# Values, bits and logits in four 32-column tiles of the matrix engine, sums turned by block transposes, 12 code rows a head, and a new order

## The chip, the cores and the metric

The kernel runs on one core of a Trainium2 chip. The metric is the device time of one execution in microseconds (us); the median of three runs before the change is 448.5 us (448.18 to 450.23). One further execution was profiled, and all rows below are from it. The engines are PE (the matrix engine; PEld is its weight load), DVE (vector), ACT (scalar), POOL (GpSimd) and SP, whose queue issues all DMAs.

## The reference

The program is three stages on 2 x 8 heads of 768 tokens with 64 columns each.

```
# attention with hashed buckets, per head
q_bits, k_bits = (q @ proj > 0), (k @ proj > 0)        # 6 bits a token
mask   = bucket(q_bits) == bucket(k_bits)
scores = where(mask, q @ k.T / 8, -1e9)
attn   = softmax(scores);  out = attn @ v
# soft mixture of experts, x is 1536 x 512, 32 slots of 8 experts
logits = x @ phi                                       # softmax over tokens, and over slots
slots  = softmax(logits, axis 0).T @ x
slots  = relu(slots @ w1[e]) @ w2[e]
x      = softmax(logits, axis 1) @ slots
# feed-forward, 512 -> 2048 -> 512
h = x @ w_in;  out = (h * sigmoid(1.702 h)) @ w_out
```

## The kernel before

Attention is written as one long list of steps, the string `ATTENTION`. Each word names a function, a head, a block of 128 keys (or queries) and a half of 384 queries, and is issued in that order. Every engine takes its own instructions in the order in which they stand, so the list sets the order on all engines and on SP's queue. A second string, `MISC`, gives each small PSUM tile one of two banks. SP's queue holds the loads of raw (q and k of a head, transposed), v, the expert weights (w), pieces of w_in, and the small moves inside SBUF.

The steps of one head n are these.

- `bits` (L390) projects q and k on the six directions, fp32, into PSUM `bp`: two column tiles of 64, one a half of 384 tokens. For head 0 (L396) q and k are projected on their own. `bits2` (L379) makes code rows of it on DVE: a threshold, then a factor. `bits3` (L372) moves these rows by four DMAs of 32 x 384 from `Bt` into rows 64 to 95 of `QK2`. The codes are such that the product of the code rows of q and k adds a large negative number for every bit that differs. They take 24 rows, so that the product that uses them has 88 rows.
- `a` (L448) multiplies queries by keys with the code rows, and DVE takes the maximum of each query (L455). `mrow` and `mstore` (L488) bring these maxima into one more row of `QK2`.
- `c` (L496) and `s` (L504) add up the scores in PSUM from split high and low parts; `e` (L509) takes the exponential on ACT into P; `p` (L517) adds the P of the key blocks on POOL into `Ps`.
- `av` (L523) multiplies v by P, fp32: two column tiles of 64, one a half of queries. Six key blocks add up in PSUM.
- `sum` (L554) multiplies `Ps` by ones, four column tiles of 32 with 384 queries each for a pair of heads; ACT copies it (L558), `rec` (L563) turns it with three PE transposes, and DVE takes the reciprocals.
- `xtok`, `xp`, `xn` turn and scale the output into rows of x. `xT` turns x again, and `lg` (L655) multiplies it by phi: two column tiles of 32 with 384 tokens each for a pair, and DVE adds it into `LT` (L657, L659), where 64 partitions hold one batch's 768 tokens in two halves.

A product in fp32 shows as two records a tile; the record counts below are such. `spin` steps are products without use at the start. After the attention list the buffers of attention are given to further expert weights (L223), and the expert stage, at whose head the logits are put together (L773), and the feed-forward stage follow.

Of the kernel before, what the change touches and what calls it, by code (L numbers as in the profile page):

```python
# [47 lines left out]
a.1.0 p.0.2.0 hi2.2.0 av.0.0 e.0.2.1 e.0.1.1 c.0.5.0 c.0.4.1 a.1.1 s.0.4.1 win.1 w4.0 we.1.1 p.0.1.1 we.1.2 w1.1 raw.3
bits3.2 hi2.2.1 av.0.1 s.0.5.0 we.1.3 e.0.5.0 w2.1 a.1.2 w3.1 av.0.2 c.0.5.1 p.0.3.0 e.0.3.1 c.0.4.0 mr.1 hq.1 e.0.4.1
a.2.1 ms.1 s.0.4.0 bits.3 p.0.2.1 bits2.3 s.0.5.1 lo1.2.1 e.0.4.0 a.2.0 av.0.3 av.0.4 vs.1 hi2.3.1 mp.1 p.0.3.1  # L50
bits3.3 a.2.2 c.1.0.1 lo2.2.1 e.0.5.1 s.1.0.1 av.0.5 a.2.4 hi2.3.0 c.1.3.0 s.1.3.0 win.2 p.0.4.1 lo1.2.0 c.1.0.0
e.1.0.1 v.2 s.1.0.0 c.1.1.0 w4.1 s.1.1.0 e.1.3.0 avo.0 c.1.2.0 e.1.1.0 p.0.4.0 a.2.3 e.1.0.0 s.1.2.0 c.1.1.1 lo2.2.0
s.1.1.1 e.1.2.0 c.1.2.1 we.2.0 we.2.1 s.1.2.1 c.1.4.1 s.1.4.1 hi1.2.1 a.2.5 p.0.5.1 av.1.0 e.1.2.1 e.1.1.1 c.1.3.1
c.1.4.0 raw.4 p.1.1.0 mr.2 p.1.1.1 s.1.3.1 p.1.2.1 w1.2 s.1.4.0 w2.2 p.1.2.0 e.1.3.1 e.1.4.0 e.1.4.1 w3.2 a.3.4
lo1.3.0 av.1.1 p.1.3.0 av.1.2 av.1.3 lo1.3.1 a.3.5 c.1.5.0 s.1.5.0 c.1.5.1 p.0.5.0 hq.2 ms.2 s.1.5.1 e.1.5.0 c.2.0.0
s.2.0.0 hi2.4.1 e.1.5.1 lo2.3.0 we.2.2 c.2.1.1 hi1.3.1 a.3.1 av.1.4 lo2.3.1 w4.2 hq.3 p.1.3.1 bits.4 bits2.4 p.1.4.1
e.2.0.0 mp.2 a.3.2 c.2.1.0 p.1.4.0 s.2.1.0 s.2.1.1 e.2.1.0 phi c.2.5.0 av.1.5 e.2.1.1 avo.1 s.2.5.0 a.3.0 e.2.5.0
c.2.0.1 s.2.0.1 win.3 we.2.3 e.2.0.1 c.2.5.1 c.2.3.0 s.2.5.1 w1.3 e.2.5.1 raw.5 p.1.5.0 vs2.0 bits3.4 p.2.1.0 s.2.3.0
e.2.3.0 p.1.5.1 hi2.4.0 c.2.2.0 a.3.3 s.2.2.0 av.2.0 w2.3 av.2.1 bits.5 v.3 w3.3 nom.0 c.2.3.1 e.2.2.0 a.4.2 s.2.3.1
c.2.4.0 c.2.2.1 s.2.2.1 mr.3 e.2.3.1 s.2.4.0 c.2.4.1 p.2.1.1 s.2.4.1 e.2.2.1 p.2.2.1 a.4.3 av.2.2 p.2.2.0 vs.2 ms.3  # L60
lo1.4.0 av.2.3 e.2.4.0 e.2.4.1 av.2.4 hi2.5.0 bits2.5 av.2.5 c.3.1.0 a.4.0 we.3.0 hi1.4.1 s.3.1.0 lo2.4.0 e.3.1.0
c.3.0.0 sum.0 s.3.0.0 p.2.3.0 p.2.4.0 a.4.4 c.3.3.1 p.2.3.1 nom.1 w4.3 c.3.3.0 e.3.0.0 p.2.4.1 xtok.0 bits3.5 s.3.3.0
# [1213 lines left out]
```

## Time and profile before

| | |
|---|---|
| median of three runs | 448.5 us (448.18 to 450.23) |
| the profiled execution | 447.2 us, its span 445.4 us |
| PE busy | 433.7 us, 97% of the span |
| DVE busy | 306.0 us, 69% |
| ACT busy | 284.9 us, 64% |
| POOL busy | 218.9 us, 49% |
| DMA | 75.09 MB, mean 169 GB/s |

The span runs from the first to the last instruction; the rest of the execution's time lies around it. Attention ends near 241 us, the expert stage near 285, and the feed-forward stage takes the remainder. A busy PE counts overlapping records once, with ends that are modelled, so starts are the safer thing to read.

### The profile page before, as it was taken

What the parts mean: (1) busy time and instruction counts of PE and PEld (TensorE: products, weight loads), DVE (VectorE), ACT (ScalarE), POOL (GpSimd) and SP (SyncE); (2) the same over time, 40 slices, a digit from 0 to 9 for tenths busy, and PEclk for the clock granted to TensorE, in tenths of its full rate; (3) what the DMA queues carried; (4) which work ended last, traced back from release to release, by engine and by line L of the source; (5) the groups of instructions that cost most, each with busy time, mean ns of one, the idle gap of its engine ahead of it and who ended that gap; (6) DMA issues with size and microseconds to landing.
All of it is one profiled execution on the core that took longest, in us unless ns stands there. A gap on an engine that the chain in (4) does not pass through costs nothing.

```text
span 445.4 us, 7076 instructions
## 1 busy us (share of the span) xinstructions
PE 433.7 (97%) x2409; PEld 292.6 (66%) x2409; DVE 306.0 (69%) x526; ACT 284.9 (64%) x578; POOL 218.9 (49%) x237
## 2 busy tenths in 40 slices
PE   8899999999999999998999999999999999999996
PEld 6556666656666666666676433467787888888885
DVE  4788788878887988888776324597876756445441
ACT  7487878879678797787673204375766646445441
POOL 5566697885686968849894000434555410000000
PEclk9999999999999999999999999999999999999999
DMA  7637446566363763663559999998000003001001
GB/s 251 204 103 237 136 137 209 178 198 212 108 211 123 219 190 121 193 206 104 167 163 418 389 408 406 405 418 337 2 0 2 0 1 141 0 1 71 0 2 71
DMA packets 28072, 75.09 MB, mean 169 GB/s; under 512 B 3882, under 2 KB 9476, under 8 KB 24452
## 3 DMA queue, kind: packets, MB, share of 16 engines
q1 hardware_dynamic: 28036, 74.64, 48.5%
q8 instruction: 19, 0.31, 0.3%
q14 instruction: 17, 0.14, 0.1%
HBM read 64.29 MB, written 7.34 MB: 161 GB/s over the span
## 4 chain that ended last, share of the span: by engine, by line
PE 76%; DMA 8%; DVE 5%; POOL 3%; ACT 3%; issue 1%; SPq 1%; ACTq 0%; DVEq 0%; POOLq 0%
PE o L1152 29%; PE av L523 11%; DMA w<-in_w 7%; PE b L496 7%; PE a L448 6%; PE b L504 6%; POOL Ps L517 3%; PE h L1124 3%; PE bp L390 2%; DMA wif<-in_w_in 1%; PE idle L200 1%; PE lg L655 1%; PE sm L554 1%; ACT P L509 1%; DVE mx L442 1%
## 5 line engine op out<-in xcount | busy, mean ns | idle before, releaser
L517 POOL TENSOR_TENSOR Ps<-Ps,P 128x384 f32<-128x384 f32 x120 | 118.8, 1007 | 12.1 <-ACT P L509 9.7
L1152 PE MATMUL o<-wh,ring 128*128 128x512 f32 x384 | 110.0, 395 | 0.6 <-DVE cT L915 0.6
L509 ACT ACTIVATE P<-b 128x384 f32<-128x384 f32 x192 | 87.4, 490 | 28.8 <-PE b L504 21.8
L455 DVE TENSOR_REDUCE MX<-a 128x1 f32<-128x768 f32 x90 | 85.7, 952 | 25.3 <-PE a L448 23.9
L1152 PEld LDWEIGHTS o<-wh,ring 128*128 128x128 f32 x384 | 71.0, 188 | 15.6 <-issue 1.4
L523 PE MATMUL av<-P,v 128*64 128x384 f32 x384 | 72.1, 497 | 0.0
L496 PE MATMUL b<-QK 128*128 128x384 f32 x192 | 66.0, 372 | 1.9 <-ACT P L509 1.7
L1133 DVE TENSOR_TENSOR XH<-h,XH 128x384 f32<-128x384 f32 x64 | 35.3, 556 | 46.3 <-ACT XH L1129 46.2
L504 PE MATMUL b<-QK 89*128 89x384 f32 (+1 forms) x192 | 62.1, 355 | 0.0
L1152 PE MATMUL o<-wl,ring 128*128 128x512 f32 x192 | 55.3, 394 | 0.0
L1129 ACT ACTIVATE XH<-h 128x384 f32<-128x384 f32 x64 | 31.3, 491 | 29.8 <-PE h L1124 29.4
L448 PE MATMUL a<-QK 88*128 88x384 f32 x180 | 49.6, 356 | 0.4 <-DVE MX L455 0.4
L496 PEld LDWEIGHTS b<-QK 128*128 128x128 f32 x192 | 35.0, 188 | 20.2 <-ACT P L509 10.7
L1138 ACT CAST ring<-XH 128x384 fp32r<-128x384 f32 x64 | 32.7, 513 | 23.0 <-DVE XH L1133 21.8
L523 PEld LDWEIGHTS av<-P,v 128*64 128x64 f32 x384 | 24.6, 136 | 29.6 <-issue 27.1
L517 POOL TENSOR_TENSOR Ps<-P,P 128x384 f32<-128x384 f32 x30 | 30.2, 1010 | 26.5 <-ACT P L509 26.4
L1152 PEld LDWEIGHTS o<-wl,ring 128*128 128x128 f32 x192 | 35.8, 188 | 10.5 <-issue 2.5
L504 PEld LDWEIGHTS b<-QK 89*128 89x128 f32 (+1 forms) x192 | 35.7, 190 | 8.0 <-issue 7.8
L1143 DVE TENSOR_TENSOR ring<-XH,ring 128x384 fp32r<-128x384 f32 x64 | 38.3, 603 | 0.3
L448 PEld LDWEIGHTS a<-QK 88*128 88x128 f32 x180 | 30.2, 189 | 12.0 <-DVE MX L455 6.5
L953 POOL TENSOR_TENSOR wl<-XH,wh 128x512 fp32r<-128x512 f32 x16 | 22.5, 1405 | 29.4 <-ACT wh L948 29.2
L241 POOL TENSOR_SCALAR wof<-wof 128x512 int32<-128x512 uint16 x16 | 11.6, 725 | 43.6 <-DMA wof<-in_w_out 42.6
(171 smaller groups left out, 575.8 us busy)
## 6 DMA issues: line engine op xcount, KB each, us to landing
w<-in_w SPq DMA_DIRECT2D x18, 1024.0 KB
w<-in_w SPq DMA_DIRECT2D x56, 256.0 KB
wif<-in_w_in SPq DMA_DIRECT2D x16, 512.0 KB
wof<-in_w_out SPq DMA_DIRECT2D x7, 1024.0 KB
raw<-in_qk SPq DMA_DIRECT2D x15, 384.0 KB
win<-wn SPq DMA_DIRECT2D x16, 256.0 KB
v<-in_v SPq DMA_DIRECT2D x16, 192.0 KB
win<-win SPq DMA_DIRECT2D x3, 1024.0 KB
```

The source lines that it names most:

```text
L448: T.matmul(a[:, h, 0:HS], q2[0:88, 0, i * 128 : (i + 1) * 128], q2[0:88, 1, h * HS : (h + 1) * HS], start=True, stop=True,)
L455: V.tensor_reduce(out=MX[:, n % 2, i : i + 1], in_=a[:, :, 0:HS], axis=AX.XY, op=ALU.max)
L496: T.matmul(b, q1[:, 1, kt * 128 : (kt + 1) * 128], q1[:, 0, h * HS : (h + 1) * HS], start=True, stop=False)
L504: T.matmul(b, q2[rows, 1, kt * 128 : (kt + 1) * 128], q2[rows, 0, qs], start=False, stop=True)
L509: A.activation(out=Pt[n, kt][:, h * HS : (h + 1) * HS], in_=bps[n, kt, h], func=AF.Exp, scale=0.125)
L517: e.tensor_tensor(out=Ps[n][:, c], in0=Pt[n, 0][:, c] if kt == 1 else Ps[n][:, c], in1=Pt[n, kt][:, c], op=ALU.add)
L523: T.matmul(avp[n][64 * h : 64 * h + 64, :], vt[n][:, kt, :], Pt[n, kt][:, h * HS : (h + 1) * HS], start=kt == 0, stop=kt == KT - 1,)
L1129: A.activation(out=gt[i], in_=hp[i], func=AF.Sigmoid, scale=1.702)
L1133: V.tensor_tensor(out=gt[i], in0=hp[i], in1=gt[i], op=ALU.mult)
L1138: A.copy(out=gh[i], in_=gt[i])
L1143: (e or V).tensor_tensor(out=gl[i], in0=gt[i], in1=gh[i].bitcast(F32), op=ALU.subtract)
L1152: T.matmul(op[grp, t], u[i][:, t * 128 : (t + 1) * 128], w[wq][:, wi, :], start=f == 0 and j == 0, stop=f == NF - 1 and j == 2,)
```

## The change

- `bits` of heads 1 to 15 becomes four column tiles of 32 with a quarter (192) of the tokens each. `bits2` then works on 192 columns.
- The codes of a head become 12 rows for q and 12 for k: six bits by the projection and six by its negative, which DVE makes at the start (`neg`). A row of constants takes up the rest; the product with codes has 77 rows, and with the maxima 78. The two constant rows are filled once a buffer: `rows` moves them for the buffers of heads 1 and 2. `bits3` moves 12 x 192 pieces, eight DMAs a head.
- `av` becomes four column tiles of 32: two halves of queries by two halves of the 64 columns of v.
- `sum` multiplies `Ps` by ones in such an order of tokens that a transpose of 32 x 32 blocks on DVE puts the sums of tokens on their partitions. ACT's copy and the PE transposes of `rec` are left out.
- `lg` becomes four column tiles of 32 with 192 tokens each, and `LT` is used as 128 partitions by two batches of 192. At the head of the expert stage eight small products with the identity put it together, where two did.
- `ATTENTION` and `MISC` are written anew.

```diff
+CROW = 64 + 2 * NBIT
+QS = S // 4
+PT = 2 * NBIT + 32
+PW = PT + 4
-idle.0 spin.6 bits.0 hi2.0.1 we.0.0 code.1.1 code.1.0 code.0.0 hi1.0.0 hi2.0.0 we.0.1 hi1.1.0 hi1.0.1 lo.0.1 spin.4
+idle.0 spin.6 hi1.0.0 we.0.0 hi2.0.1 lo.0.0 neg.1 neg.0 neg.2 bits.0 code.1.1 hi2.0.0 code.1.0 code.0.0 spin.3 bits.1
...
+    LT2 = LT.rearrange("p (b c) -> p b c", b=2)
...
+    def negate(t, r, first, k):
+        w = t[r, first : first + 4 * NBIT].rearrange("p (k x b) -> p k x b", k=2, x=2)
+        V.tensor_scalar(out=w[:, k, 1, :], in0=w[:, k, 0, :], scalar1=-1.0, scalar2=None, op0=ALU.mult)
...
     def bits(n):
...
-        for h in (0, 1) if n else ():
-            T.matmul(
-                bp[0][64 * h : 64 * h + 64, :], prj[:, 0:64], raw[n][:, h * HS : (h + 1) * HS], start=True, stop=True
-            )
+        if n:
+            Bt[n] = misc([128, QS], f"bp{n}")
+            for g in range(4):
+                T.matmul(
+                    Bt[n][32 * g : 32 * g + 32, :],
+                    prj[:, 0:32],
+                    raw[n][:, g * QS : (g + 1) * QS],
+                    start=True,
+                    stop=True,
+                )
+            return
...
     def bits3(n):
-        for h in range(2):
+        for g in range(4):
             for s in range(2):
-                c = 64 * h + 32 * s
-                move(QK2[n % 3][64:96, s, h * HS : (h + 1) * HS], Bt[n][c : c + 32, :])
+                c = 32 * g + 2 * NBIT * s
+                move(QK2[n % 3][64:CROW, s, g * QS : (g + 1) * QS], Bt[n][c : c + 2 * NBIT, :])
...
+    def rows(n):
+        move(QK2[n][CROW : CROW + 2, :, :], QK2[0][CROW : CROW + 2, :, :])
...
     def av(n, kt):
...
-        for h in range(2):
+        for c in range(4):
+            h, d = c // 2, c % 2 * 32
             T.matmul(
-                avp[n][64 * h : 64 * h + 64, :],
-                vt[n][:, kt, :],
+                avp[n][32 * c : 32 * c + 32, :],
+                vt[n][:, kt, d : d + 32],
                 Pt[n, kt][:, h * HS : (h + 1) * HS],
...
     def sums(p):
-        ps = misc([128, HS], f"sm{p}")
-        for c in range(4):
-            n, h = 2 * p + c // 2, c % 2
-            T.matmul(
-                ps[32 * c : 32 * c + 32, :], ones[:, 0:32], Ps[n][:, h * HS : (h + 1) * HS], start=True, stop=True
-            )
-        sms[p] = ap.tile([128, HS], F32, name=f"sms{p}", tag="tmp", bufs=1)
-        A.copy(out=sms[p], in_=ps)
+        ps = misc([128, 2, KT, 32], f"sm{p}")
+        for a in range(2):
+            rows = Ps[2 * p + a].rearrange("p (t g i) -> p t g i", t=KT, g=4)
+            for g in range(4):
+                T.matmul(ps[32 * g : 32 * g + 32, a, :, :], ones[:, 0:32], rows[:, :, g, :], start=True, stop=True)
+        sms[p] = ap.tile([128, 2, KT, 32], F32, name=f"sms{p}", tag="tmp", bufs=1)
+        V.transpose(sms[p].rearrange("p a t i -> p (a t i)"), ps.rearrange("p a t i -> p (a t i)"))
 
     def recs(p):
-        tp = misc([128, 3, 128], f"smt{p}")
-        for t in range(3):
-            T.transpose(tp[:, t, :], sms[p][:, t * 128 : (t + 1) * 128], ident)
-        recip(2 * p, 2, [tp.rearrange("p t (c r) -> p c t r", r=32)[:, :, :, 0]])
+        recip(2 * p, 2, [sms[p][:, :, :, 0].rearrange("p a (h t) -> p (a h) t", h=2)])
...
     def logits(p):
...
-        for hf in range(2):
-            r = 64 * b + 32 * hf
-            T.matmul(ps[r : r + 32, :], phs[:, c, :], xTs[p, hf], start=True, stop=True)
+        for g in range(4):
+            x = xTs[p, g // 2][:, g % 2 * QS : (g % 2 + 1) * QS]
+            T.matmul(ps[32 * g : 32 * g + 32, :], phs[:, c, :], x, start=True, stop=True)
```

PE around the bits of head 9, before: the bits (bp9) stand inside a group of values (av6), and the first product with head 9's codes (a9) comes 23 rows behind them.

```order
L523 MATMUL av6_1337<-P6_3_1275,v6_1202 64x384 x2
L390 MATMUL bp9_1410<-raw9_1302,prj_102 64x384 x2
L523 MATMUL av6_1337<-P6_4_1376,v6_1202 64x384 x2
L523 MATMUL av6_1337<-P6_5_1363,v6_1202 64x384 x2
L504 MATMUL b7_0_0_1378<-QK2_1_88 128x384
...
L504 MATMUL b7_3_0_1486<-QK2_1_88 128x384
L504 MATMUL b7_5_0_1504<-QK2_1_88 128x384
L448 MATMUL a9_5_1509<-QK2_0_94 128x384 x2
```

The same place after the change.

```order
L527 MATMUL b6_3_1_1471<-QK1_0_92 128x384
L547 MATMUL av6_1452<-P6_1_1428,v6_1285 32x384 x4
L402 MATMUL bp9_1481<-raw9_1425,prj_102 32x192 x4
L471 MATMUL a8_0_1492<-QK2_2_91 128x384 x2
L519 MATMUL b6_5_1_1497<-QK1_0_92 128x384
...
L527 MATMUL b7_3_1_1654<-QK1_1_95 128x384
L485 MATMUL mtp8_1666<-cst_66,MX_103 128x128
L471 MATMUL a9_5_1671<-QK2_0_94 128x384 x2
```

The bits of head 9 now stand earlier, behind the second step of the values of head 6 instead of the fourth, and 38 rows lie between them and the first product with their codes.

SP's queue around the same head's code rows (Bt9), before: raw is the next head's q and k, v its values, w expert weights, wif and win32 pieces of w_in, mr the row of maxima.

```order
L678 DMA win32_3_78<-wn7_1354 128x512
L372 DMA QK2_0_94<-Bt9_1417 32x384 x4
L321 DMA v8_1453<-in_v 128x384
L225 DMA w7_1458<-in_w1 128x512 x2
L315 DMA raw10_1490<-in_qk 128x768
L225 DMA w7_1458<-in_w1 128x512 x2
L488 DMA QK2_2_91<-mr8_1521 1x6x128
```

The same place after the change.

```order
L231 DMA w7_1474<-in_w1 128x512
L378 DMA QK2_0_94<-Bt9_1488 12x192 x8
L332 DMA wif8_1610<-in_w_in 128x1024
L697 DMA win32_3_78<-wn7_1516 128x512
L327 DMA v8_1645<-in_v 128x384
L321 DMA raw10_1659<-in_qk 128x768
L231 DMA w7_1474<-in_w1 128x512
```

Eight pieces stand where four stood, and two transfers of w_in are now between them and the next v and raw.

DVE at the start, before: the first thresholds (bpk, bp) make the codes of head 0.

```order
L192 MEMSET LT_68 128x128
L193 MEMSET bz_70 128x1
L379 TENSOR_SCALAR QK2_0_94<-bpk_122,raw0_85 32x384 x2
L379 TENSOR_SCALAR QK2_0_94<-bp0_121,raw0_85 32x384 x2
L428 MEMSET mx0_147 128x6
```

The same place after the change.

```order
L198 MEMSET LT_68 128x128
L199 MEMSET bz_70 128x1
L389 TENSOR_SCALAR raw0_85<-raw0_85 64x6 x2
L389 TENSOR_SCALAR prj_102<-prj_102 128x2x6
L385 TENSOR_SCALAR QK2_0_94<-bpk_130,raw0_85 32x384 x2
L385 TENSOR_SCALAR QK2_0_94<-bp0_129,raw0_85 32x384 x2
L451 MEMSET mx0_150 128x6
```

Three small negations, the last one on prj, now stand ahead of the thresholds.

## Rows read from the trace of the kernel before

**Rows 1.** Busy time by stage (stretch; length; engines with records; PEclk, DMA share, GB/s).
```profile
30.00:230.00 200.00, 196.74 (x1107) 125.58 (x1106) 166.22 (x261) 158.58 (x320) 153.51 (x170) 1.00 0.55 169
256.00:310.00 54.00, 52.66 (x383) 27.05 (x376) 31.18 (x55) 23.96 (x54) 12.83 (x13) 1.00 1.00 406
```

**Rows 2.** The chain that ended last, share of the span by engine.
```profile
PE 76%; DMA 8%; DVE 5%; POOL 3%; ACT 3%; issue 1%; SPq 1%; ACTq 0%; DVEq 0%; POOLq 0%
```

**Rows 3.** PE in order of time, head 9's bits (start us, us, then the instruction).
```profile
115.81 0.87 PE L523 MATMUL av<-P,v 128*64 128x384 f32 x4
116.50 0.82 PE L390 MATMUL bp<-raw,prj 128*64 128x384 f32 x4
117.15 1.46 PE L523 MATMUL av<-P,v 128*64 128x384 f32 x8
118.54 0.45 PE L504 MATMUL b<-QK 89*128 89x384 f32 x1
...
124.01 0.52 PE L448 MATMUL a<-QK 88*128 88x384 f32 x2
```

**Rows 4.** PE in order of time: sums, their transposes, a lone value group, logits.
```profile
83.28 0.85 PE L554 MATMUL sm<-Ps,cst 128*32 128x384 f32 x8
84.06 0.45 PE L496 MATMUL b<-QK 128*128 128x384 f32 x1
...
87.91 0.50 PE L563 MATMUL smt<-cst,sms 128*128 128x128 f32 x3
88.17 0.42 PE L496 MATMUL b<-QK 128*128 128x384 f32 x1
...
121.36 0.87 PE L523 MATMUL av<-P,v 128*64 128x384 f32 x4
122.15 0.62 PE L448 MATMUL a<-QK 88*128 88x384 f32 x2
...
189.16 0.84 PE L655 MATMUL lg<-xT,phs 128*32 128x384 f32 x4
189.93 0.45 PE L496 MATMUL b<-QK 128*128 128x384 f32 x1
```

**Rows 5.** Groups of PE by line (records; busy us, mean ns; idle before).
```profile
L390 PE MATMUL bp<-raw,prj 128*64 128x384 f32 x60 | 12.6, 497 | 0.6 <-DMA raw<-in_qk 0.6
L655 PE MATMUL lg<-xT,phs 128*32 128x384 f32 x28 | 5.9, 498 | 0.0
L563 PE MATMUL smt<-cst,sms 128*128 128x128 f32 x21 | 3.4, 273 | 0.0
```

**Rows 6.** PE in order of time, slots of the expert stage.
```profile
250.81 1.50 PE L822 MATMUL sps<-XH,etile 128*32 128x256 f32 x24
```

**Rows 7.** Groups of DVE by line.
```profile
L379 DVE TENSOR_SCALAR Bt<-bp,prj 128x384 fp32r<-128x384 f32 x14 | 9.4, 669 | 0.5 <-PE bp L390 0.5
L659 DVE TENSOR_TENSOR LT<-lg,LT 64x384 f32<-64x384 f32 x5 | 2.7, 549 | 0.1
```

**Rows 8.** SP's queue in order of time, head 9's code rows and what follows.
```profile
118.39 2.44 SPq L372 DMA_DIRECT2D QK<-Bt  x4
...
124.98 0.33 SPq L315 DMA_DIRECT2D raw<-in_qk  x1
```

**Rows 9.** All issues of code rows (duration ns min/median/max, first and last start).
```profile
L372 SPq DMA_DIRECT2D QK<-Bt x60: 512/582/1672, 10.6 to 205.7; - x60
```

**Rows 10.** Start: SP, DVE and PE in order of time.
```profile
2.60 0.43 SPq L332 DMA_DIRECT2D prj<-in_qk  x1
...
5.40 1.39 DVE L379 TENSOR_SCALAR QK<-bpk,raw 32x384 fp32r<-32x384 f32 x2 [4.41 <-PE bpk L396]
...
6.85 0.87 PE L390 MATMUL bp<-raw,prj 128*64 128x384 f32 x4
```

**Rows 11.** SP's queue, first loads into attention's buffers.
```profile
229.34 4.40 SPq L223 DMA_DIRECT2D w<-in_w  x4
```

More of the change, by code (lines that the diff above doesn't have):

```diff
@@ L48 @@
[L48 to L62, printed above, removed]
@@ L138 @@
-e.15.5.0 we.13.2 xg.14 e.15.5.1 p.15.3.1 p.15.4.1 p.15.4.0 w4.15 we.13.3 av.15.3 av.15.4 p.15.5.1 p.15.5.0 av.15.5
-sum1.15.0 avo.15 xtok.15 xadd.15 sum1.15.1 xn1.15
+idle.0 spin.6 hi1.0.0 we.0.0 hi2.0.1 lo.0.0 neg.1 neg.0 neg.2 bits.0 code.1.1 hi2.0.0 code.1.0 code.0.0 spin.3 bits.1
+code.0.1 hq.0 spin.1 a0.0 hi1.0.1 lo.0.1 a0.4 we.0.1 we.0.2 a0.2 bits2.1 rows.1 raw.2 bits3.1 w1.0 a0.3 spin.1 a0.1
+a0.5 w2.0 hi2.1.0 hi1.1.0 c.0.3.0 hi1.1.1 mred.0 a0.8 hi2.1.1 lo.1.1 spin.3 a0.6 a0.7 spin.3 mr0.0 w3.0 spin.1 a0.11
@@ new lines @@
+a0.9 mr1.0 s.0.3.0 hq.1 c.0.0.0 e.0.3.0 bits.2 spin.2 c.0.2.0 hi2.2.0 lo.1.0 a0.10 s.0.2.0 s.0.0.0 c.0.1.0 s.0.1.0
+bits2.2 mred.1 hi2.2.1 e.0.0.0 we.0.3 v.1 e.0.2.0 a.1.3 vs.0 e.0.1.0 p.0.1.0 we.1.0 c.0.1.1 mr0.1 spin.1 a.1.4 mr1.1
+rows.2 c.0.0.1 s.0.1.1 s.0.0.1 c.0.2.1 e.0.1.1 e.0.0.1 win.1 s.0.2.1 a.1.0 lo1.2.0 bits3.2 c.0.4.1 vs.1 e.0.2.1 w4.0
+raw.3 p.0.1.1 we.1.1 p.0.2.0 c.0.3.1 s.0.4.1 s.0.3.1 c.0.5.0 e.0.3.1 s.0.5.0 e.0.4.1 a.1.1 c.0.4.0 we.1.2 av.0.0 a.1.2
+we.1.3 lo2.2.0 av.0.1 w1.1 e.0.5.0 p.0.2.1 s.0.4.0 c.1.0.1 a.1.5 av.0.2 mp.1 c.0.5.1 w2.1 s.0.5.1 hi1.2.1 p.0.3.0 mr.1
@@ L694, in build @@
     todo = {
-        "idle": idle0, "spin": spins, "bits": bits, "bits2": bits2, "bits3": bits3, "hi2": hi2, "hi1": hi1, "hq": hq,
+        "idle": idle0, "spin": spins, "bits": bits, "bits2": bits2, "bits3": bits3, "rows": rows, "neg": neg, "hi2": hi2, "hi1": hi1, "hq": hq,
         "lo": lo, "lo1": lo1, "lo2": lo2,
@@ L770, in build @@
     lg = mm([128, HS], "lg")
-    for r in range(2):
-        rs = slice(64 * r, 64 * r + 64)
-        T.matmul(lg[rs, :], ident[:, rs], LT, start=True, stop=r == 0)
+    for q in range(2):
+        for r in range(4):
+            rs = slice(64 * (r % 2) + 32 * q, 64 * (r % 2) + 32 * q + 32)
+            T.matmul(
+                lg[32 * r : 32 * r + 32, q * QS : (q + 1) * QS],
+                ident[:, rs],
+                LT2[:, r // 2, :],
+                start=q == 0,
+                stop=r < 2 and q == 1,
+            )
     idle[0] = mps.tile([128, 128], F32, name="idle1", tag="idle", bufs=1)
```

253 lines of the change are left out of this document (134 added, 119 removed).

## The prediction

> **What bounds the kernel now.** I read the busy time by stage first, then the chain, then PE's own order of time. By stage, PE is busy for 196.7 of the 200 us between 30 and 230 us, and DVE, ACT and POOL for 166, 159 and 154 [rows 1]. The chain agrees: 76% of the span is PE [rows 2]. A busy PE could still wait inside a group, so I checked the starts: in the stretch at 116 us each group begins where the one before leaves off [rows 3]. So in attention, time taken off PE is time off the span, as long as the three engines at 77 to 83% can follow. The stretch behind it is bound elsewhere: from 256 to 310 us the DMA share is 1.00 [rows 1]. The loads that fill it are issued from 229.34 us on [rows 11], as attention's buffers come free, so that stretch moves with the end of attention and does not swallow the gain. The feed-forward part behind it is not touched.
>
> **The change on PE.** Durations are start to start.
>
> Bits. One head's projection between two value groups takes 117.15 - 116.50 = 0.65 us [rows 3]: two 64-column tiles side by side, two passes of 384 columns. After the change four 32-column tiles take 192 columns each, so each pass is half as long. That four tiles run side by side at full rate is seen in the sums: eight records of 384 columns in 84.06 - 83.28 = 0.78 us, the switch into and out of tiles included [rows 4]. Halved, 0.65 becomes 0.33. The nearest row with short passes is 24 records of 256 columns in 1.50 us, six passes of 0.25 [rows 6]; two of these, 0.50, are the upper end. 60 records, four a head, are 15 heads [rows 5]. The saving is 15 x 0.32 = 4.8 us; at the upper end of the price 2.2.
>
> Logits. A pair takes 189.93 - 189.16 = 0.77 us [rows 4], also two passes of 384, now of 192: 0.32 less. 28 records are 7 pairs [rows 5], so 2.2 us; by the same bound 1.0.
>
> Sums. They keep their size: eight products of 192 columns in four tiles are two rounds, as long as four of 384. What goes is three PE transposes a pair: 88.17 - 87.91 = 0.26 us [rows 4], times 7 (21 records [rows 5]), 1.8 us. The moving operand of the sums is now read in runs of 32 columns with gaps; no row shows such a read. At half rate it would cost 7 x 0.65 = 4.6 us; I take full rate, at which every fp32 group in rows 3 and 4 runs, and keep the other end for the range.
>
> Values. Four tiles of 32 columns do what two of 64 did, and each still streams 384 columns twice: no fewer passes. A lone group takes 122.15 - 121.36 = 0.79 us, the sums with four tiles 0.78 [rows 4], so I count 0.01 to 0.02 for each of some 50 groups: 0.8 us. If four streams at once were slower than two, the sums would show it.
>
> Together 4.8 + 2.2 + 1.8 + 0.8 = 9.6 us; 5.8 with the upper price of short passes, 5.0 with half-rate sums, about 1 with both. The two orders hold 59 and 60 groups of tiled products, so the switches stay.
>
> **The other engines.** DVE: 14 threshold steps of 669 ns [rows 7] have half the columns; between 335 and 669 ns I take 470, 2.8 us less. Seven block transposes of 128x384 out of PSUM are new, and no row shows one: work of that many columns out of PSUM takes 549 (logit addition) to 669 ns (threshold) [rows 7]; at 0.6 they add 4.2 us. The logit additions go from 384 to 192 columns, 7 x 0.2 = 1.4 less. DVE nets zero: 166 of some 191 us, 87%. ACT loses seven copies. No total becomes the bound; for the crowding on DVE I allow 0.5 us, 0 to 2.
>
> At the start DVE negates the projection's columns, and the third of these steps works on prj, ahead of the first thresholds in DVE's order. Those start at 5.40 us; prj is in issue until 3.03 and first used at 6.85 [rows 10]. So the thresholds come 0 to 1.6 us later, and the two negations ahead of the first bits act in the same place. I take 0.5: the start is a chain through DVE. Queued behind are the first row maxima, for which PE waits.
>
> **The wait that the change adds.** The code rows reach QK2 through SP's queue. At head 9 four issues took 2.44 us [rows 8]; the median of one is 582 ns and the longest 1672 [rows 9]. Eight take 4.9, so 2.4 us more for each of 15 heads. Before, 124.01 - 120.83 = 3.2 us lay between the last issue's end and the first product that needs the codes [rows 3, 8]. At the same distance, and with bits 0.3 and threshold 0.2 us shorter, 1.3 us would be left for the landing. But the order gives more room. Between bits and that product of head 9 stand 23 rows of PE before and 38 after; the 23 took 124.01 - 117.15 = 6.9 us [rows 3], 0.30 us a row. Over all 15 heads the mean is 28.9 rows before and 31.6 after, the shortest 21 and 27. From the end of the bits to the end of the last issue it was 120.83 - 117.15 = 3.7 us, and will be 5.9. So the mean head keeps 9.5 - 5.9 = 3.6 us for the landing, the shortest 2.2, and a head whose threshold waits on DVE can be short. I take 1.0 us lost in all, 0 to 6. Behind the eight pieces queue the next v, raw and w_in tiles and the row of maxima; before, raw was issued only at 124.98 us, 4 us after head 9's codes [rows 8], so SP has room.
> The Trainium skill (DMA: Bandwidth & Descriptors, Anatomy of one DMA) speaks against splitting a transfer: it gives each a fixed cost of about 2.0 us whatever its size, for the software path, while these go from SP. By that figure a head at the old distance would come 0.7 us late, some 10 us in 15 heads, and the gain would be gone; the trace of before, in which 3.2 us were left, does not contradict it.
>
> **Sum.** 9.6 - 0.5 (crowding) - 0.5 (start) - 1.0 (late codes) = 7.6 us off the profiled run of 447.2 us (a span of 445.4 and 1.8 around it): 439.6. The median of the runs shown is 448.5, 1.3 above the profiled one; 448.5 - 7.6 = 440.9, so 441. Its own range is 438 to 444.
>
> **Rivals.**
> 1. More comes through. The order is new throughout, and the 3.3 us in which PE was idle between 30 and 230 us [rows 1] may shrink too. For it: nothing but PE is at its limit. Against: the old order had closed almost every gap [rows 3]. 9.6 + 3 off: 436.
> 2. Most is eaten by codes that come late or by a crowded DVE: for it the eight issues on one queue and DVE at 87%; against it the longer distance. With 3 us left, or none, 445 to 448.
> 3. Slower. One mechanism: the first maximum product of a head stands in PE's order ahead of all the rest, so if the codes land late, PE waits with everything behind it, 15 times. It decides at 9.6 / 15 = 0.64 us late a head; at 1 us it costs 15, and the time is 448.5 - 9.6 + 15 = 454. For it: issues of up to 1.67 us [rows 9]. Against: the shortest distance grew from 21 to 27 rows, some 1.8 us.
> 4. The change does not do what it says: the halved passes stay long, because eight weight loads do not keep up with 0.33 us, and bits and logits pay the price of [rows 6]. For it: no row has a pass under 256 columns in tiles. Against: nothing there points to a floor. 5.8 less the 2.0 of losses: 445.
>
> **How the numbers follow.** Forecast 0.60, rival 1 0.13, rivals 2 and 4 together 0.19, rival 3 0.08. The range takes in rival 1 and the lower half of rivals 2 and 4: 436 to 447, which leaves out about 0.16. 0.5% is 2.2 us, about what a measurement of this kernel can tell from no change. Below 446.3: the forecast, rival 1 and about half of 2 and 4, 0.82. Within: 0.10. Above 450.7: 0.08.
>
> **What would show it.** Right: bits at 0.33 us between neighbours, no PE transposes of the sums, logits near 0.45 with the switches, value groups as long as before, the loads of 229.34 us now near 222, and the rest of the program shifted by as much. Wrong: PE idle ahead of a head's first maximum product, released by a DMA; sums longer than 0.78 us; block transposes far over 0.67 us; DVE as PE's releaser in the middle stretch; the first thresholds after 6 us.

## The result and the profile after

The changed kernel takes 451.85 us (median of 20 runs, 448.8 to 454.82); on the same chip the kernel before took 448.68. The ratio is 1.0072, with a 95% interval of 1.0047 to 1.0096: slower by 0.5 to 1%, where 441 was predicted. Its profiled execution took 448.8 us, the shortest of the 20 (a span of 446.5 us); the one of the kernel before was 447.2 (445.4). So the traces show 1.1 us of the 3.2 between the medians; the rest is in no trace.

The busy time by stage of the changed kernel (stretch; length; PE, PEld, DVE, ACT, POOL with records; PEclk, DMA share, GB/s) answers to [rows 1]:

```profile
0.00:30.00 30.00, 24.75 (x137) 17.17 (x137) 18.16 (x34) 19.47 (x31) 13.83 (x17) 0.89 0.51 156
30.00:230.00 200.00, 192.26 (x1584) 122.70 (x1581) 170.20 (x269) 156.05 (x312) 154.44 (x171) 1.00 0.53 166
```

PE is idle for 7.7 us between 30 and 230 us, where it was for 3.3, and for 5.3 in the first 30. DVE has 4 us more to do, though it was to stay equal. The chain, by engine, says the same:

```profile
PE 66%; DMA 13%; DVE 9%; ACT 5%; SPq 3%; issue 2%; POOL 2%; ACTq 0%; DVEq 0%; POOLq 0%
```

PE has fallen from 76% [rows 2]; DMA, DVE and SP's queue have taken its place.

PE's own parts came out as worked out. PE in order of time, head 5's bits and the lone sums of the first pair, answers to [rows 3, 4]:

```profile
60.44 0.53 PE L402 MATMUL bp<-raw,prj 128*32 128x192 f32 x8 [0.21 <-DMA raw<-in_qk]
60.76 0.85 PE L547 MATMUL av<-P,v 128*32 128x384 f32 x8
61.55 0.44 PE L519 MATMUL b<-QK 128*128 128x384 f32 x1
...
53.94 0.86 PE L579 MATMUL sm<-Ps,cst 128*32 128x192 f32 x16
54.73 0.62 PE L519 MATMUL b<-QK 128*128 128x384 f32 x2
```

Bits take 0.32 us from start to start (0.65 before), a lone value group 0.78 to 0.79 and the sums 0.79, with no PE transposes behind them. In one experiment below (three parts alone) lone logits took 0.46 us instead of 0.77. PE's busy time in all falls from 433.7 to 427.1 us, a stretch of 6.8 us at half clock (see the start below) included, and to 424.4 in the best version below. So nearly all of the 9.6 us were spared, and lost again elsewhere. PE's waits in the changed kernel (what waits, for what: us in all, times, longest) show where to look:

```profile
PE a L471 <- DVE MX L478: 2.4, 4, 1.1
PE bp L402 <- DVE QK L385: 2.3, 1, 2.3
PE bp L402 <- DMA raw<-in_qk: 2.2, 4, 1.2
PE b L527 <- DMA QK<-mr: 1.5, 2, 1.0
```

The weight load of `a` alone waited 11.9 us for MX, DVE's row maxima (6.5 before). Three places stand out.

**The start.** POOL and DVE in order of time, which answers to [rows 10]:

```profile
5.74 3.74 POOL L360 TENSOR_TENSOR QK<-raw,QK 64x768 fp32r<-64x768 f32 x2 [3.92 <-ACT QK L351]
6.38 1.20 DVE L389 TENSOR_SCALAR prj<-prj 128x12 f32<-128x12 f32 x1 [1.45 <-DMA prj<-in_qk]
7.59 1.37 DVE L385 TENSOR_SCALAR QK<-bpk,raw 32x384 fp32r<-32x384 f32 x2
```

The third negation waits for prj until 6.38 us and then takes 1.20 us; the two on raw, of six columns, took 0.16 and 0.17. It ends at 7.58; the first of POOL's two steps, which ran all that time, ended at 7.55. The thresholds start 2.2 us later than before, head 1's bits too, at 9.02 us, and the thresholds are what PE waits for there (2.3 us in the list above). The granted clock is 0.5 (1.2 GHz) from 10.8 to 17.6 us, behind a stretch from 6 to 10 us in which PE was busy for 1.67 of 4; before, it was 1.00 there. The first maximum product of head 1 comes at 21.62 us instead of 17.85. This is one execution; at the start they differ (below).

**SP's queue.** Code rows of all heads (duration ns min/median/max, first and last start), and head 9's pieces with the next raw in order of time; they answer to [rows 9] and [rows 8]:

```profile
L378 SPq DMA_DIRECT2D QK<-Bt x120: 713/714/911, 11.8 to 209.4; - x120
```

```profile
115.30 6.34 SPq L378 DMA_DIRECT2D QK<-Bt  x8
...
123.26 0.43 SPq L321 DMA_DIRECT2D raw<-in_qk  x1
```

The median issue was 582 ns, and is 714 for a piece half as wide. With the gaps a head's eight take 6.2 us, and all issues of SP between 30 and 230 us add up to 135 us, 88 before.

**DVE's small steps.** The groups of DVE answer to [rows 7]; the last two had means of 247 ns and, with one operand in PSUM, 171 ns before:

```profile
L385 DVE TENSOR_SCALAR Bt<-bp,prj 128x192 fp32r<-128x192 f32 x14 | 5.7, 410 | 2.2 <-PE bp L402 1.4 <-DMA w<-in_w 0.8
L581 DVE STREAM_TRANSPOSE sms<-sm 128x384 f32<-128x384 f32 x7 | 4.0, 578 | 1.5 <-PE sm L579 1.5
L602 DVE TENSOR_SCALAR rec<-nma 128x12 f32<-128x12 f32 (+1 forms) x9 | 4.3, 480 | 0.0
L606 DVE TENSOR_TENSOR rec<-sms,rec 128x12 f32<-128x12 f32 x7 | 3.3, 476 | 0.2
```

Threshold and block transpose are a little shorter than estimated (470 and 600). The steps on 12 columns behind the transposes are not: they run 0.16 to 0.93 us. POOL and DVE in order of time show why:

```profile
117.86 0.82 POOL L615 TENSOR_TENSOR nv<-vsb,nma 128x384 f32<-128x384 f32 x1
118.15 0.56 DVE L602 TENSOR_SCALAR rec<-nma 128x12 f32<-128x12 f32 x1
118.65 1.00 POOL L540 TENSOR_TENSOR Ps<-Ps,P 128x384 f32<-128x384 f32 x1
118.75 0.93 DVE L606 TENSOR_TENSOR rec<-sms,rec 128x12 f32<-128x12 f32 x1
```

Each begins inside a POOL step and ends 0.03 us after it. The first of the two steps, on nma, read and wrote SBUF before the change too, and two of its seven were held then (0.63 and 0.47 us); in the new order it is five of seven. Only the second, the addition, has got its operand moved from PSUM to SBUF: three of seven are held, and none was. Against 0.16 and 0.18 us the held steps lose 2.9 and 2.1 us of DVE.

### The profile page after: what moved, and what is told of

Its sections match the earlier page's. It is cut to its first block, busy times and chain, and to the rows that moved or that the text cites. A ratio compares the mean times of both kernels' runs of the same rounds, so it can differ in the third digit from the quotient of the medians.

```text
span 446.5 us, 8235 instructions
## 1 busy us (share of the span) xinstructions
PE 427.1 (96%) x2926; PEld 290.4 (65%) x2926; DVE 308.9 (69%) x536; ACT 282.1 (63%) x571; POOL 216.5 (48%) x237
## 4 chain that ended last, share of the span: by engine, by line
PE 66%; DMA 13%; DVE 9%; ACT 5%; SPq 3%; issue 2%; POOL 2%; ACTq 0%; DVEq 0%; POOLq 0%
PE o L1178 29%; PE av L547 9%; DMA w<-in_w 7%; PE b L519 5%; PE a L471 5%; PE b L527 5%; DMA raw<-in_qk 3%; DVE MX L478 3%; PE h L1150 3%; ACT P L532 2%; SPq L378 2%; POOL Ps L540 2%; PE bp L402 1%; DMA wif<-in_w_in 1%; DMA QK<-mr 1%
## 5 line engine op out<-in xcount | busy, mean ns | idle before, releaser
L532 ACT ACTIVATE P<-b 128x384 f32<-128x384 f32 x192 | 86.2, 489 | 29.4 <-PE b L527 26.0
L478 DVE TENSOR_REDUCE MX<-a 128x1 f32<-128x768 f32 x90 | 85.6, 951 | 19.8 <-PE a L471 18.3
L547 PE MATMUL av<-P,v 128*32 128x384 f32 x768 | 74.0, 492 | 0.0
L519 PE MATMUL b<-QK 128*128 128x384 f32 x192 | 67.0, 370 | 1.0 <-ACT P L532 0.9
L527 PE MATMUL b<-QK 78*128 78x384 f32 (+1 forms) x192 | 62.1, 352 | 1.5 <-DMA QK<-mr 1.5
L471 PE MATMUL a<-QK 77*128 77x384 f32 x180 | 50.3, 360 | 2.5 <-DVE MX L478 2.4
L1164 ACT CAST ring<-XH 128x384 fp32r<-128x384 f32 x64 | 32.7, 513 | 23.4 <-DVE XH L1159 22.2
L519 PEld LDWEIGHTS b<-QK 128*128 128x128 f32 x192 | 35.9, 190 | 15.1 <-ACT P L532 6.6
L471 PEld LDWEIGHTS a<-QK 77*128 77x128 f32 x180 | 29.8, 189 | 17.0 <-DVE MX L478 11.9
L527 PEld LDWEIGHTS b<-QK 78*128 78x128 f32 (+1 forms) x192 | 35.8, 190 | 7.5 <-issue 5.3
L547 PEld LDWEIGHTS av<-P,v 128*32 128x32 f32 x768 | 21.4, 109 | 26.2 <-issue 22.6
L1169 DVE TENSOR_TENSOR ring<-XH,ring 128x384 fp32r<-128x384 f32 x64 | 37.2, 585 | 1.3 <-ACT ring L1164 1.0
L979 POOL TENSOR_TENSOR wl<-XH,wh 128x512 fp32r<-128x512 f32 x16 | 22.6, 1411 | 31.0 <-ACT wh L974 30.8
```

What stands on the lines that cost most here:

```text
L471: T.matmul(a[:, h, 0:HS], q2[0:CROW + 1, 0, i * 128 : (i + 1) * 128], q2[0:CROW + 1, 1, h * HS : (h + 1) * HS], start=True, stop=True,)
L478: V.tensor_reduce(out=MX[:, n % 2, i : i + 1], in_=a[:, :, 0:HS], axis=AX.XY, op=ALU.max)
L519: T.matmul(b, q1[:, 1, kt * 128 : (kt + 1) * 128], q1[:, 0, h * HS : (h + 1) * HS], start=True, stop=False)
L527: T.matmul(b, q2[rows, 1, kt * 128 : (kt + 1) * 128], q2[rows, 0, qs], start=False, stop=True)
L532: A.activation(out=Pt[n, kt][:, h * HS : (h + 1) * HS], in_=bps[n, kt, h], func=AF.Exp, scale=0.125)
L547: T.matmul(avp[n][32 * c : 32 * c + 32, :], vt[n][:, kt, d : d + 32], Pt[n, kt][:, h * HS : (h + 1) * HS], start=kt == 0, stop=kt == KT - 1,)
```

## The experiments

Each time is a median; the ratio is to the kernel before on the same chip in the same session. The runs come from several chips, so a gain between two of them can differ by up to 1.5 us as it is taken from the medians or from the ratios; where that matters both are given.

### The count of moves

Four moves of 32x384 a head cut into eight of 32x192, all else as before:

```diff
-move(QK2[n % 3][64:96, s, h * HS : (h + 1) * HS], Bt[n][c : c + 32, :])
+for z in (0, S // 4):
+    move(QK2[n % 3][64:96, s, h * HS + z : h * HS + z + S // 4], Bt[n][c : c + 32, z : z + S // 4])
```

> The kernel before, with each move of code rows cut in two: eight DMAs of 32 x 192 a head in place of four of 32 x 384, nothing else. Theory A (the eight pieces on SP's queue cost the change its gain: the issue of codes grows by some 2.5 to 3.5 us a head, raw, maxima and codes come late): slower by 4 us or more, and in its trace PE waits for raw, QK<-mr or codes in the middle stretch. Rival B (the loss is in the new order, in DVE or at the start, and SP has room): within 1.5 us of before.

Measured: 457.52, ratio 1.0189 (1.0149 to 1.0228), 9.2 us over the kernel before. Four more issues a head cost 0.6 us a head with nothing else changed.

The other way round, the changed kernel with four moves (the edit in words):

```diff
-bits: tile g = token quarter g, weights prj[:, 0:32], 192 columns
+bits: tile g = half g // 2, operand g % 2, weights prj[:, 12 * s : 12 * s + 32], 384 columns
-8 moves of 12 x 192
+4 moves of 12 x 384
```

> The changed kernel with the bits in four 32-column tiles by half and operand instead of by token quarter: four passes of 384 columns, so that a head's codes take four moves of 12x384 again, not eight of 12x192. PE pays the 4.8 us that the quarters saved (15 x 0.32), the threshold step is 384 columns long again (14 x about 0.2 = 2.8 us of DVE). Theory A (the eight issues on SP's queue, 0.77 us each, hold up codes and loads): the queue gets back 60 issues; at the 9.2 us that four more moves a head cost the kernel before, 451.9 - 9.2 + 4.8 = 447.5, and PE's waits for raw and for the row of maxima shrink from 3.7 us to under 2. Rival B (the start, the clock and the order cost the gain, not the queue): 451.9 + 4.8 = 456 or more, with the same waits for the start and for DVE.

Measured: 449.14, ratio 1.0000 (0.9975 to 1.0025). PE pays 4.8 us more and the time falls by 2.4 against the kernel before, so eight moves instead of four had cost about 7.2 (8.0 by the ratios), although the threshold steps are 384 columns long again. PE's waits for raw and for the row of maxima have left the list of its ten longest.

### The order

> The changed kernel's steps in the order of the kernel before (negations and the two moves of constant rows put in where they are needed). Theory A and C (the new way of moving codes and the start cost the gain, the order does not): about as slow as the changed kernel or slower, 450 to 456, since the old order leaves less room between bits and the first product with codes. Rival D (the new order is worse than the old one): 439 to 446, the 9.6 us of PE come through in part.

> The kernel before, its steps in the order of the changed kernel (no negations, four moves of codes a head; two of the seven reciprocal steps a few places earlier, since their PSUM bank would else not come free). Theory A and C: as before within 3 us (446 to 452), no long PE waits for DMAs in the middle, no late start. Rival D (the order is worse): 453 or more.

Measured: 471.14 (ratio 1.0491, 1.0446 to 1.0536) and 462.74 (1.0316, 1.0282 to 1.0350). PE's longest waits in the new code in the old order, and then in the old code in the new order:

```profile
PE bp L410 <- DMA raw<-in_qk: 5.6, 4, 3.0
PE a L479 <- DVE MX L486: 5.5, 7, 2.1
PE a L479 <- DMA QK<-Bt: 3.1, 6, 0.8
```

```profile
PE xtp L614 <- DVE rec L595: 4.3, 5, 2.2
```

Neither came out as theories A and C had it (450 to 456, and 446 to 452): the second lies where rival D, a worse order, put it, and the first, far above rival D's 439 to 446, speaks against it. Each order fits its own code only. In the old one the code rows come late six times, and the new code is 19 us slower in it than in the new one. What the new order costs or gains by itself can't be read from code that it wasn't made for; that stays open.

Next, three parts alone in the old order, with old bits and moves; and the same with values in two 64-column tiles again (in words):

```diff
+logits by token quarters; sums turned by DVE           (both)
+values in four 32-column tiles                          (first only)
```

> The kernel before in its own order, bits, codes and four moves, with three parts of the change alone: logits by token quarters, values in four 32-column tiles, sums turned by DVE block transposes. PE is spared 2.2 + 0.8 + 1.8 = 4.8 us, SP's queue and the start are as before. Theory A (the parts on PE are worth what they save; the queue ate it): 448.3 - 4.8 = 443.5. Rival (an order written for one set of lengths loses as much elsewhere: DVE holds seven block transposes of about 0.6 us more, and the engines that must follow are late): 447 to 450.

> The kernel before in its own order, with the logits by token quarters and the sums turned by DVE, values as before in two 64-column tiles. With values in four 32-column tiles the same kernel took 449.95, and each of its 11 stretches in which values stand beside bits was 0.14 to 0.18 us longer than before (3.65 for 3.38, 2.22 for 2.09 us), where bits still use 64-column tiles. Theory M (tiles of two widths side by side cost a switch): 15 heads x 0.14 = 2 us come back, and 45 groups of values lose 0.6: 448.5. Rival (the loss of that kernel is DVE's alone, which holds the transposes): 450 or more.

Measured: 449.95 (1.0036, 1.0013 to 1.0058) and 447.71 (1.0008, 0.9986 to 1.0030). So theory A's 443.5 is refuted for the first. The second is as theory M expects, but the two intervals overlap, and its switch is shown by the traces. PE in order of time around head 14's bits, with narrow and then with wide values:

```profile
186.47 0.85 PE L526 MATMUL av<-P,v 128*32 128x384 f32 x8
187.26 0.87 PE L392 MATMUL bp<-raw,prj 128*64 128x384 f32 x4
188.05 2.14 PE L526 MATMUL av<-P,v 128*32 128x384 f32 x24
190.12 0.62 PE L450 MATMUL a<-QK 88*128 88x384 f32 x2
```

```profile
185.61 0.87 PE L525 MATMUL av<-P,v 128*64 128x384 f32 x4
186.31 0.82 PE L392 MATMUL bp<-raw,prj 128*64 128x384 f32 x4
186.95 2.11 PE L525 MATMUL av<-P,v 128*64 128x384 f32 x12
188.99 0.62 PE L450 MATMUL a<-QK 88*128 88x384 f32 x2
```

The same work takes 3.65 us with two changes of tile width in it and 3.38 with none: 0.14 a change. In the changed kernel bits and values have one width, so that doesn't arise there. The second kernel still gains nothing from logits and sums (4.0 us on PE). Either work taken from PE in an order made for other lengths is not time, or DVE's seven block transposes and longer additions (0.39 us in the mean in the first of these kernels, 0.17 before) cost as much; no run here parts the two.

### The rows of a move

Four zero rows are added to each code tile, so that a move carries 16 rows:

```diff
-CROW = 64 + 2 * NBIT
+CROW = 64 + 16
-move(QK2[n % 3][64:CROW, s, ...], Bt[n][c : c + 2 * NBIT, :])     # c = 32 * g + 2 * NBIT * s
+move(QK2[n % 3][64:CROW, s, ...], Bt[n][c : c + 16, :])           # c = 32 * g + 16 * s
```

> The changed kernel with one edit: 16 rows in each of its eight moves a head instead of 12, the third negation on DVE as in the change. Theory (the two costs add, 5.0 for the rows and 3.4 for the negation): 451.9 - 5.0 = 446.9, an issue of 0.59 us instead of 0.71, a head's eight issues 5.3 us instead of 6.2. Rival (16 rows help only where the start is not late): 449 to 450.

Measured: 446.76, ratio 0.9959 (0.9940 to 0.9978): 5.1 us less than the change by the medians, as expected, with one edit that adds rows. Two more kernels bring 28 rows to the kernel before, and 16 to the kernel with four moves and the third negation on ACT (which follows below):

> The kernel before with 28 rows in each of its four moves a head instead of 32 (the rows left out are not read). If an issue is dearer wherever the rows don't fill all 16 DMA engines evenly: 0.71 us instead of 0.58, as with 12 rows, a head's four issues 3.2 us instead of 2.6, and 448.3 to 450. If it goes by the count of rows: 0.59 to 0.61 us and 448.3.

> The kernel with four moves a head and the negation on ACT, but each code tile has four zero rows more, so that a move carries 16 rows of 384, not 12. Moves of 32 rows were issued in 0.58 us (384 columns) and 0.59 (192 columns), moves of 12 rows in 0.71 to 0.72 whatever their length. Theory R (an issue is dearer where the rows don't fill all 16 DMA engines): 0.58 us here, 60 x 0.14 = 8 us of SP's queue back; at the price that the queue had so far (60 issues more cost 7.5 to 9.2 us, some 0.2 us for each us of queue) 445.7 - 1.7 = 444. Rival (it goes by the number of rows, or by another difference of the two layouts): 0.72 or between, and 445.7.

Measured: 448.60 (1.0013, 0.9994 to 1.0031) and 445.69 (0.9961, 0.9939 to 0.9984). The issues, first with 28 rows in the kernel before, then with 16 in the change (in the kernel with eight moves of 32x192 above the median was 588 ns):

```profile
L372 SPq DMA_DIRECT2D QK<-Bt x60: 746/752/996, 10.6 to 206.8; - x60
```

```profile
L379 SPq DMA_DIRECT2D QK<-Bt x120: 507/587/1374, 11.8 to 206.7; - x120
```

16 and 32 rows take 0.58 to 0.59 us with 192 and with 384 columns, 12 rows 0.71 to 0.72 with either, and 28 rows 0.75 with 384: it isn't the count of rows, and theory R stands for the issue. The Trainium skill (DMA: Bandwidth & Descriptors, Why a DMA increments its semaphore by 16 and not by 1) says that a DMA is spread over the largest number of engines up to 16 that divides its rows, and that the issuing sequencer itself writes the increments of the engines left out. These four sizes agree with that (16, 16, 12 and 14 engines); no run here shows the engines. With four moves a head the shorter issue was worth nothing (445.69 for 445.71, and not theory R's 444): there the queue has room. It is worth 5 us with eight.

Moving half of the pieces to ACT's queue was the other way out:

> The changed kernel with four of a head's eight code moves (the rows of q's codes) issued from ACT's queue instead of SP's. SP is spared 60 issues of 0.77 us. If SP's queue is the cost and an issue on ACT is short or falls into ACT's idle fifth: 451.9 - 5 to 9 = 443 to 447, PE's waits for raw and codes under 1.5 us. If an issue holds ACT as long as it holds SP (60 x 0.77 = 46 us more on an engine that is busy 156 of 200 us) ACT becomes the limit: 455 to 470, with PE waiting for P and for rounded operands from ACT.

Measured: 479.70, ratio 1.0706 (1.0662 to 1.0751). That is worse than either expectation. An issue is as long from ACT as from SP; in the 45.1 us of the 60 issues ACT computes for 13.9, and PE waits for P:

```profile
L439 ACTq DMA_DIRECT2D QK<-Bt x60: 726/736/1321, 11.8 to 234.1; - x60
```

```profile
PE b L521 <- ACT P L534: 14.9, 11, 2.5
```

### DVE beside POOL

The third negation by ACT, alone and with four moves or 16 rows:

```diff
-V.tensor_scalar(out=w[:, :, 1, :], in0=w[:, :, 0, :], scalar1=-1.0, ...)
+A.activation(out=w[:, :, 1, :], in_=w[:, :, 0, :], func=AF.Copy, scale=-1.0)
```

> The changed kernel, with the third negation (on prj) done by ACT instead of DVE, so that the first thresholds do not stand behind it. Theory C (part of the loss is the start: thresholds from 7.59 instead of 5.40 us, PE idle 2.3 us, the granted clock halved from 10.8 to 17.6 us): the first thresholds near 5.8 us, no half clock, first maximum product of head 1 two to three us earlier than 21.6, and 2 to 4 us off the whole. Rival (the start is regained later by slack): under 1 us off.

> The same four moves, and the third negation (12 columns of prj) done by ACT instead of DVE. If the start and the queue are two separate costs they add: 3.4 us less than the kernel with four moves alone, so 444 by theory A and 452 by rival B. If the start's delay is only absorbed later, the same as with four moves alone.

> The changed kernel with its eight moves a head by token quarters, the third negation on ACT, and moves of 16 rows of 192 instead of 12. Against the same with 12 rows (448.4): by theory R 120 x 0.14 = 16 us of SP's queue back, 445, and PE's waits for raw and codes gone but for about 1 us; against four moves a head of 16 rows PE is 4.8 us better and SP 35 us worse, so about the same as that. Rival (the count of issues is what matters, not their length): 448.

Measured: 448.41 (1.0012, 0.9981 to 1.0043), 445.71 (0.9945, 0.9920 to 0.9971) and 443.44 (0.9919, 0.9889 to 0.9950). In all three the time falls by 3.3 to 3.4 us by the medians against the same kernel with the negation on DVE (451.85, 449.14 and 446.76), and by 2.7, 2.5 and 1.8 by the ratios. The start of the first, in order of time:

```profile
5.69 1.37 DVE L385 TENSOR_SCALAR QK<-bpk,raw 32x384 fp32r<-32x384 f32 x2 [0.42 <-PE bpk L415]
6.07 3.73 POOL L360 TENSOR_TENSOR QK<-raw,QK 64x768 fp32r<-64x768 f32 x2 [4.25 <-ACT QK L351]
6.69 0.21 ACT L396 ACTIVATE prj<-prj 128x12 f32<-128x12 f32 x1
```

The thresholds start 1.9 us earlier, beside a running POOL step that doesn't hold ACT's 0.21 us. But in this execution four products on PE took 1.49 us at 4.15 us where the changed kernel's took 0.83, and two took 0.99 at 15 us: twice as long up to 19 us, as at the lower clock, although its rows give a granted clock of 1.00 there. So its first maximum product of head 1 was no earlier (22.2 for 21.6 us), and the first pair of traces doesn't show the expected gain. The other two pairs do: 21.2 to 19.8 us with four moves, 22.6 to 19.0 with 16 rows. How PE's first 20 us run differs from execution to execution.

The small steps behind the block transposes on POOL instead of DVE, with four moves, with eight of 16 rows, and with eight but the last pair left on DVE:

```diff
 def recip(n, k, parts):
+    e = G if k == 2 else V            # last version: if k == 2 and n < 12
-    V.tensor_scalar(out=rf, ...); V.tensor_tensor(out=r, in0=x, in1=r, ...)
+    e.tensor_scalar(out=rf, ...); e.tensor_tensor(out=r, in0=x, in1=r, ...)
```

> The kernel with four moves a head and the negation on ACT, but the two small steps behind each block transpose (128x12, from and to SBUF) run on POOL instead of DVE. In the changed kernel these took up to 931 ns on DVE when they began inside a POOL step and ended with it, 160 to 180 ns else; 14 of them lost some 5 us of DVE against one lot of 0.8 us before, when one operand was still in PSUM. Theory P (DVE and POOL keep each other out of SBUF, and DVE's lost time holds up the row maxima PE waits for): PE's weight loads for a, which waited 12.5 us for MX, wait less by 1 to 3, and the time is 444 to 445. Rival: the waits lie elsewhere and nothing changes (445.7), or POOL's queue holds the steps back (447).

> The eight moves of 16 rows with the third negation on ACT (443.4), and the two small steps behind each block transpose on POOL instead of DVE. With four moves a head they gave 445.7 - 444.7 = 1.0 us. Theory P (DVE's lost time holds up row maxima, wherever the codes come from): 442.4. Rival (with the shorter bits POOL is the nearer limit): 443.4 to 444.5.

> Eight moves of 16 rows, third negation on ACT, small steps behind the block transposes on POOL for all pairs but the last, whose steps stay on DVE. If the wait of 1.5 us for them is what drops the clock at 226 us and gives the lead back: no half clock there, the loads of the stretch behind still at 221, and 444.7 - 3.5 = 441, the predicted time. Rival (the lead of 8.6 us is lost in another way at the end of attention, whatever the clock): 443 to 444.5.

Measured: 444.68 (0.9928, 0.9895 to 0.9961), 444.73 (0.9915, 0.9886 to 0.9944) and 440.11 (0.9837, 0.9804 to 0.9870). The first two can't be told from the kernels they were made of, 445.71 and 443.44. But the trace of the second was ahead by as much as the prediction had asked for: its first load into attention's buffers stands at 220.72 us (229.34 [rows 11]; the second line is the change's, 229.89):

```profile
220.72 12.56 SPq L230 DMA_DIRECT2D w<-in_w  x5
```

```profile
229.89 5.00 SPq L229 DMA_DIRECT2D w<-in_w  x4
```

It lost the lead at the end of attention. POOL, DVE and PE there, and the stretches around it:

```profile
223.60 0.21 POOL L611 TENSOR_TENSOR rec<-sms,rec 128x12 f32<-128x12 f32 x1
223.85 0.23 DVE L613 RECIPROCAL rr<-rec 128x12 f32<-128x12 f32 x1 [2.46 <-POOL rec L611]
225.27 0.80 PE L596 MATMUL sm<-cst,Ps 128*128 128x1 f32 x6 [1.47 <-DVE XH L641]
```

```profile
222.00:226.00 4.00, 2.53 (x19) 2.27 (x18) 2.08 (x5) 2.56 (x7) 2.97 (x7) 1.00 0.92 266
226.00:230.00 4.00, 4.00 (x18) 3.90 (x18) 2.91 (x8) 1.36 (x3) 1.56 (x2) 0.55 1.00 393
```

The last pair's steps queue behind other work on POOL, PE stands idle for 1.47 us, is busy for 2.53 of 4, and then runs at the lower level (1.2 GHz, PEclk 0.55) for nearly 7 us. In the third kernel the last pair's steps are on DVE, and the same stretches read:

```profile
222.00:226.00 4.00, 4.00 (x41) 3.31 (x32) 3.00 (x8) 2.33 (x7) 4.00 (x6) 1.00 0.82 207
226.00:230.00 4.00, 4.00 (x30) 3.91 (x30) 3.65 (x9) 2.82 (x8) 2.36 (x3) 1.00 0.95 368
```

No half clock follows, and 441, the predicted time, is there: 440.11. Its loads start at 222.98 us, 6.4 ahead of the kernel before, not 8.6 as expected, but nearly all of that stays: its span is 6.0 us shorter (439.4 for 445.4), the second kernel's 4.4 (441.0). The two differ only in where the last pair's steps run. Last, what the turn of the sums is worth (two `rec` steps stand a few places earlier here, so that a PSUM bank is free):

> The eight moves of 16 rows with the third negation on ACT (443.4), but the sums copied by ACT and turned by three PE transposes a pair as in the kernel before. PE pays 1.8 us, ACT seven copies of about 0.5; DVE is spared seven transposes of 0.58 and what its small steps lost to POOL, some 8 us in all. If PE's time decides: 445.2. If the waits for the row maxima on DVE decide: 443.4 or less.

Measured: 455.90, ratio 1.0158 (1.0124 to 1.0191), some 12 us more than with the turn, which neither side expected. PE waits 4.6 us in `xtp` for `rec`, as the old code did in the new order, so the run prices the old sums in this order, not the turn by itself; that stays open.

### The clock at the start

Six idle products are put into PE's wait for the first row maxima:

```diff
-a0.3 spin.1 a0.1 a0.5
+a0.3 spin.1 a0.1 spin.6 a0.5
```

> The same with six more idle products of PE (128 columns, some 1.2 us in all) in the 1.4 us that it waits for the row maxima of head 0 at 9.5 us. If the half clock of 3.4 us from 11 to 15 us follows that gap, it goes, and the time falls by 0.5 to 1.5 us; if it doesn't, or these products come in the way of the chain, the same or 0.5 us more.

Measured: 438.06, ratio 0.9800 (0.9763 to 0.9836), the best version; without the products 440.11 on the same chip, though the two intervals overlap. Stretches without and with them:

```profile
8.00:11.00 3.00, 1.64 (x9) 1.19 (x8) 2.86 (x7) 2.48 (x5) 2.71 (x3) 1.00 0.79 290
11.00:15.00 4.00, 3.95 (x18) 3.73 (x19) 3.31 (x7) 3.93 (x6) 0.45 (x2) 0.59 0.44 132
```

```profile
8.00:11.00 3.00, 2.75 (x20) 2.37 (x19) 2.80 (x7) 1.65 (x4) 2.31 (x2) 1.00 0.90 315
11.00:15.00 4.00, 3.96 (x27) 3.19 (x27) 3.48 (x8) 3.93 (x6) 0.23 (x1) 1.00 0.28 98
```

With PE busy for 2.75 us of the 3 the clock stays at 2.4 GHz here. The first maximum product of head 1 then comes at 18.70 us instead of 19.15, so the start explains 0.5 of the 2 us between the medians; the rest isn't explained.

## Why the prediction was wrong

- **PE's savings** were right: bits 0.32 (0.33 worked out), logits 0.46 alone, sums 0.79 and at full rate, values 0.01 less a group. No pass was held up by its weight loads, so rival 4 falls.
- **The step that failed most is "eight take 4.9"** in the wait that the change adds. It took the issue time of moves with 32 rows, 0.61 us, for moves with 12. They take 0.71, a head's eight 6.2, and the issue goes by how the rows share out, which I had not looked for. From the end of the bits to the end of the last issue a head spends 7.7 us on average, not 5.9. The longer issues are 1.3 us of that; most of the rest is that head 9 was taken for the mean head: its 3.7 us before was among the shortest, the mean of the 15 was 4.7. From the last landing to the first product that needs it there are 0.07 to 0.17 us in three heads, 1.4 in the median. Rival 3 named the right place but not the right form: the codes themselves come late for few heads.
- **"SP has room"** failed with it. What queues behind the pieces comes late too: PE waits 2.2 us for raw and 1.5 for the row of maxima. I had allowed 1.0 us for late codes; with 12 rows, eight moves instead of four cost 7.2 us. Of that 16 rows give back 5. The rest, seen from the other side: with 16 rows eight moves are 445.69 - 443.44 = 2.3 us better than four, where PE's 4.8 were spared, so 2.5 are still paid.
- **The start** was bounded by when prj is first used, 0 to 1.6 us, and taken as 0.5. The wait for prj was in that bound; that a negation of 12 columns takes 1.20 us beside POOL was not. Off DVE it gave back 3.4 us by the medians, 1.8 to 2.7 by the ratios.
- **The crowding on DVE** was taken as 0.5, 0 to 2. The large steps were right, but the two small steps of a pair wait for POOL: the addition because the sums now lie in SBUF, the other because the new order puts it beside POOL's steps more often. With all pairs but the last taken off DVE they gave 443.44 - 440.11 = 3.3 us (2.5 against the kernel before on each chip, 3.7 by the ratios). Rival 2 had a crowded DVE, but by its total; what the rows show is a step that waits for one on POOL. How much of the 3.3 is that wait and how much the steps' own work (some 2 us of DVE) no run parts.

The misses add up to (7.2 - 1.0) + (3.4 - 0.5) + (3.3 - 0.5) = 11.9 us; the result lies 451.85 - 441 = 10.9 above the forecast. By the ratios and the other ways of taking the parts the sum is 9.5 to 13 us, and the parts were measured one upon the other, not all alone; that it comes within 1 us is partly luck. The 441 itself was reached by taking these costs away, the small steps' work on DVE included, and not by any change on PE. That the best version goes 3 us under it is not explained by PE's parts; the half clock that the idle products end isn't in the kernel before's trace, and whether the new order gives the rest was not tried.

The Trainium skill (SBUF — State Buffer, SBUF: two separate sides) has the rule that I passed over: DVE and GpSimd share one pair of ports, and whichever starts first shuts the other out until it ends, when the DVE step is in a two-port mode, or has two SBUF inputs and the GpSimd step reads SBUF. This trace agrees: the negation ends with POOL's step at 7.58 us, the small steps 0.03 us behind POOL's (but one addition, at 57.14 us, ran 0.19 us beside a short POOL step and ended just ahead of it), while the same addition with one operand in PSUM took 170 to 171 ns every time before, beside POOL or not. Which of the two cases a step falls under no row shows.

## What to carry to other kernels

Before an operand moves from PSUM to SBUF, or a small step is put on DVE or moved in the order, look at what POOL runs there: a step of 0.16 us can take 0.93. Price a DMA's issue from rows of the same shape, count what queues behind it, and round the rows to 16 where that costs nothing. When PE is at its limit, work taken off it is worth its time only if the codes, loads and maxima that PE needs next also come earlier by as much; and behind one idle gap of 1.5 us there came 7 us at half clock here.
